# Shorter programs in a one-token attention and feed-forward block: K turned a tile at a time, head 0's scores as a loop, 1/L taken where o is gathered

## The chip, the core and the metric

The kernel runs on one core of a Trainium2 chip. The metric is the device time of one launch in microseconds, the median of several runs. Beside the times there is one profiled execution of the kernel; every stretch and every row below comes from that one.

## What is computed

One token (a row of 512 numbers) goes through a conditioned block: six modulation vectors from `silu(c) @ w_mod`, a layer norm, attention with 32 query heads over a cache of 8 key/value heads with 32768 positions each, an output projection, and a feed-forward part with ReLU. Almost all bytes are the cache: 8 heads x (K and V) x 32768 x 128 in bf16, 8 MB for each K and each V of a head.

```python
mod = (silu(c) @ w_mod).reshape(1, 6, 1, 512)
sa, ca, ga, sb, cb, gb = (mod[:, i] for i in range(6))
h = layernorm(x) * (1 + ca) + sa
q = (h @ wq) as 32 heads of 128; k, v: 8 heads, each for 4 query heads
p = softmax(q @ k.T * 128 ** -0.5); o = p @ v
x = x + ga * (o as a row of 4096 @ wo)
h = layernorm(x) * (1 + cb) + sb
out = x + gb * (relu(h @ w1) @ w2)
```

## The kernel before

**Loads.** `stream` is a list of loads, all issued in its order on SP's queue (`stream_dma`, line 154): first half of K of head 0, `w_mod`, `wq`, second half of K0, then K1, V0, K2, V1, K3, V2 and so on, at the end `wo` in four parts, `w1`, and `w2` in five parts. They land in a `ring` of three slots of 8 MB. A load is issued only when the slot's last reader has finished: V0 takes the slot of `w_mod` and `wq`, K2 that of K0, V1 that of K1, K3 that of V0; `tail_sb` (`wo`, `w1`, `w2`) takes the slot of the last K. `need(key)` makes the loads in the program up to the one asked for.

**A head.** A K of a head lies on 128 partitions in four tiles of 64 positions each per partition (`u` = 0 to 3), and each tile in two halves. `turn_k` transposes a half in 32 x 32 blocks in place on VectorE (DVE); `scores` runs eight matmuls of 512 columns on it (TensorE, PE), so 64 for a head, into two PSUM banks. The stationary operand is `qbd`, the four queries of the head laid out block-diagonally; `build_qbd` fills it with four ScalarE (ACT) copies. `softmax(g)` is a generator, whose steps are laid between other work: the maximum over the two banks, two small transposes on PE to spread the maximum, the exponentials on ACT with their sum `l_g`, the transpose of the probabilities on DVE, and 1/L (`Lexp`, `L_ps`, `Linv`). `pv` multiplies the probabilities with V: 64 matmuls a head, a loop on PE for heads 0 to 4 and half of head 5 (a section of its own, `tile_critical`), written out for the rest. `open_o` clears its PSUM tile. `blocks`, `o_cols`, `normalise` and `spread` gather o of a head into columns, multiply by 1/L, and lay it out for the output projection `project(i)`. Parts 0 and 1 of that projection (`WOROWS`) give rows, 1 matmul of 512 columns for each row of `wo_sb`; parts 2 and 3 give columns, 4 matmuls of one column each; `join_rows` turns the rows and adds them to the columns.

**Order.** PE's and DVE's programs stand in the order in which the code is written (`manual_schedule`). For head 0 all halves are turned, then scored, then its softmax is run to the end, and only behind it stand the turns of K1. From head 1 on, the turns and scores of head h stand ahead of the PV of head h - 1. For the last head, each of the two score banks has its own maximum (`bank_max`), and the PV of the head before is laid into the gaps. Eighteen `keep_clock` matmuls into a spare bank (line 631) stand between the steps of the tail.

Of the kernel before, what the change touches and what calls it, by code (L numbers as in the profile page):

```python
# [17 lines left out]
def kernel(  # L18
# [14 lines left out]
    nc = tc.nc  # L33
# [13 lines left out]
    WOP = [(0, Hkv // 2), (Hkv // 2, Hkv // 4), (Hkv - 2, 1), (Hkv - 1, 1)]  # L47
    WOROWS = 2
    LAST = Hkv - 1
# [28 lines left out]
    front = ctx.enter_context(tc.tile_pool(name="front", bufs=1))  # L78
    mask4 = front.tile([P, 32], F32, name="mask4_sb")[:, 0:REP]
    ring = ctx.enter_context(tc.tile_pool(name="ring", bufs=3))  # L80
# [113 lines left out]
    ib = ident_bf[:]  # L194
    for hp in range(4):
        h, par = hp // 2, hp % 2
        src = AP(ib.tensor, ib.offset + 64 * h + par, [[ib.ap[0][0], P], [0, 4], [2, 32]])
        nc.vector.tensor_copy(out=sel[:, hp, :].rearrange("p (a c) -> p a c", a=4), in_=src)
    QW = P + 4 * 7
# [5 lines left out]
    nc.vector.tensor_reduce(  # L205
        out=mask4, in_=ident_f[:].rearrange("p (x q) -> p q x", q=REP), op=ALU.add, axis=AX.X,
    )

    cmask, rsel = {}, {}
    for n in sorted({n * REP for _, n in WOP}):  # L210
        cmask[n] = const.tile([P, P // n], F32, name=f"cmask{n}")
        nc.vector.tensor_reduce(
            out=cmask[n][:], in_=ident_f[:].rearrange("p (c r) -> p c r", r=n), op=ALU.add, axis=AX.X,
        )
        rsel_f = const.tile([P, n], F32, name=f"rsel_f{n}")
        nc.vector.tensor_reduce(
            out=rsel_f[:], in_=ident_f[:].rearrange("p (c r) -> p r c", r=n), op=ALU.add, axis=AX.X,
        )
        rsel[n] = const.tile([P, n], BF16, name=f"rsel{n}")
        nc.vector.tensor_copy(out=rsel[n][:], in_=rsel_f[:])  # L220

# [38 lines left out]

    acc_ps = ps_acc.tile([P, REP + KT], F32)
    nc.vector.memset(acc_ps[:], 0.0)
    oT_ps, attnT_ps = acc_ps[:, 0:REP], acc_ps[:, REP:REP + KT]

# [63 lines left out]
    for u in range(2):  # L328
        for half in range(2):
            t = need(("k", 0, u))[:, 32 * half:32 * half + 32, :].rearrange("p j d -> p (j d)").bitcast(F32)  # L330
            nc.vector.transpose(out=t, in_=t)  # L331

    mod_b = two_banks("mod_ps")
    mod_ps = [row_bank(mod_b[:, i, :]) for i in range(2)]
    to_rows(mod_ps, siluT, wm_sb, 6)
# [51 lines left out]
    q_b = two_banks("q_ps")  # L387
    q_ps = [row_bank(q_b[:, i, :]) for i in range(2)]
    wq_f = wq_sb.rearrange("p kt (i h a e) -> p kt i a h e", i=2, a=4, e=32)
# [20 lines left out]
    def build_qbd(g):  # L410
        d_ap = qbd[g % 2][:]
        d_ps = d_ap.ap[0][0]
        s_ap = qrep_sb[:]
        s_ps = s_ap.ap[0][0]
        for a in range(4):
            o = AP(d_ap.tensor, d_ap.offset + (32 * a) * d_ps + 4 * 7 + 32 * a,
                   [[d_ps, 32], [QW, 4], [1, 4]])
            i = AP(s_ap.tensor, s_ap.offset + (32 * a) * s_ps + REP * g,
                   [[s_ps, 32], [Hq, 4], [1, 4]])
            nc.scalar.copy(out=o, in_=i)  # L420


    S_tiles, m_tiles, S_ps_tiles = {}, {}, {}
    PT_tiles, Linv_tiles = {}, {}
# [4 lines left out]
    def turn_k(g, u, half):  # L429

        if u == 0 and half == 0:
            S_tiles[g] = two_banks("S_ps")
            m_tiles[g] = spool.tile([P, NG], F32, tag="m2", name="m2")
# [5 lines left out]
        t = nc.vector.transpose(out=KTt.bitcast(F32), in_=KTt.bitcast(F32))  # L439
        behind_loop(t)  # L440
# [21 lines left out]

    def bank_max(g, G):
        behind_loop(nc.vector.reduce_max(out=m_tiles[g][:, G:G + 1], in_=S_tiles[g][:, G, :], axis=AX.X))

    def softmax(g):

        S_g, m2 = S_tiles.pop(g), m_tiles.pop(g)
        m_p = spool.tile([P, 1], F32, tag="m_p", name="m_p")
        if g < LAST:  # L470
            behind_loop(nc.vector.reduce_max(out=m_p[:], in_=S_g.rearrange("p g f -> p (g f)"), axis=AX.X))  # L471
        else:
            nc.vector.reduce_max(out=m_p[:], in_=m2[:], axis=AX.X)
        yield
# [26 lines left out]
        PT_tiles[g] = P_g  # L501
        Lexp = spool.tile([P, REP], F32, tag="Lexp", name="Lexp")
        nc.vector.tensor_scalar(out=Lexp[:], in0=mask4, scalar1=l_g[:], scalar2=None, op0=ALU.mult)  # L503
# [6 lines left out]
        Linv_tiles[g] = Linv  # L510

    def pv(g, us, js=range(16)):
# [5 lines left out]

        def step(u, V, PT, Vx):
            nc.tensor.matmul(o_tiles[g][:], lhsT=PT, rhs=Vx, start=False, stop=False, skip_group_check=True)  # L520

        Vf = [V.rearrange("p (s j) d -> p s (j d)", s=4) for V in Vs]
        if g < HALVED or g == HALVED and us[0] > 0:

            with tc.tile_critical() as section:
                last_loop[:] = loop[:] = [section.name]
                with nc.tensor.Fori(0, 512 - 32 * nb + 1, 32 * nb) as at:
                    for b in range(nb):
                        for u, V in zip(us, Vf):
                            step(u, V, PT_g[:, u // 2, 32 * b + 16 * (u % 2):][:, bass.DynSlice(at, 16)],  # L530
                                 V[:, :, Dh * b:][:, :, bass.DynSlice(at * (Dh // 32), Dh)])
        else:
# [29 lines left out]
    def normalise(g):  # L562
# [6 lines left out]
        nc.vector.tensor_tensor(  # L569
            out=oA[i][:, REP * (g - g0):REP * (g - g0 + 1), :],  # L570
            in0=o_g.unsqueeze(2).to_broadcast([P, REP, CH]),
            in1=cmask[n * REP][:].unsqueeze(1).to_broadcast([P, REP, CH]), op=ALU.mult,
        )
        PT_tiles.pop(g)
# [58 lines left out]
    with tc.manual_schedule(engines={mybir.EngineType.PE, mybir.EngineType.DVE}):  # L633
        build_qbd(0)
        for turn in (turn_k, scores):
            for u in range(NTILE):
                for half in range(2):
                    turn(0, u, half)
        open_o(0)
# [45 lines left out]
        spread(part_of(g - 1))  # L685
        bank_max(h, 0)
# [5 lines left out]
        bank_max(h, 1)  # L692
        soft = softmax(h)
# [129 lines left out]
```

## Time and profile before

| | |
|---|---|
| median of 3 timed runs | 354.26 us (354.23 to 354.55) |
| span of the profiled execution, first to last instruction | 352.6 us |
| the timed median less that span | 1.66 us |
| busy, share of the span | PE 79%, weight loads 32%, DVE 57%, ACT 7%, GpSimd (POOL) 1% |
| read from memory | 149.42 MB, 424 GB/s over the span |
| mean granted PE clock | 0.937 |

The profiled execution is shown by its span alone; the time around it is the difference to the timed median. Rows of a timeline have start, duration, engine, line, operation, tiles and count, and in brackets the idle time ahead and what ended it. `SPq` is the issuing of a transfer, not the transfer. PEld is the load of a stationary operand. In a row of windows stand the stretch, its length, the busy time of PE, PEld, DVE, ACT and POOL with the number of instructions, the granted clock, the share of DMA and the GB/s.

### The profile page before, as it was taken

How to read it: one execution, taken by the hardware profiler on the slowest of the kernel's cores; microseconds unless marked ns; L12 is line 12 of the kernel's file. 1: busy time of each engine (PE TensorE's matmuls, PEld its weight loads, DVE VectorE, ACT ScalarE, POOL GpSimd, SP SyncE). 2: the span in 40 equal slices, each digit the busy share in tenths (PEclk: the TensorE clock that was granted, in tenths of full speed). 3: DMA queues.
4: the chain of work that ended last, by engine and by line, in shares of the span. 5: the costliest groups of instructions: out<-in, count | busy, mean ns of one | idle time of the engine just before them, and what ended most of it. 6: DMA issues, size and time to landing. Idle time of an engine off the chain costs nothing. (4 is left out here: it accounts for less than half of the span.)

```text
span 352.6 us, 3715 instructions
## 1 busy us (share of the span) xinstructions
PE 277.9 (79%) x1310; PEld 113.5 (32%) x1310; DVE 201.0 (57%) x226; ACT 25.1 (7%) x69; POOL 3.1 (1%) x15
## 2 busy tenths in 40 slices
PE   0065891895998599976998499968999799989994
PEld 0021330331333234322333134323444233434442
DVE  6663564984079614974099506975684257744142
ACT  1200103002000200001000200011000100011000
POOL 2000000000000000000000000000000000000000
PEclk9999897798999879998999879996999989999999
DMA  9999989999999999999999999999999999999995
GB/s 357 398 435 452 472 388 461 454 394 454 461 394 448 439 424 439 424 433 439 416 446 446 409 440 461 411 394 454 431 414 435 457 417 420 444 439 409 425 425 214
DMA packets 5224, 149.59 MB, mean 424 GB/s; under 512 B 604, under 2 KB 988, under 8 KB 1628
## 3 DMA queue, kind: packets, MB, share of 16 engines
q1 hardware_dynamic: 5180, 149.43, 98.5%
q8 instruction: 8, 0.13, 0.1%
q14 instruction: 4, 0.03, 0.0%
q10 hardware_dynamic: 32, 0.00, 0.0%
HBM read 149.42 MB, written 0.00 MB: 424 GB/s over the span
## 5 line engine op out<-in xcount | busy, mean ns | idle before, releaser
L439 DVE STREAM_TRANSPOSE Ksb<-Ksb 128x2048 f32<-128x2048 f32 x60 | 133.1, 2276 | 60.2 <-DMA Ksb<-in_A_k_cache_dram 60.2
L520 PE MATMUL o_ps<-Vsb,P_g 128*16 (+1 forms) x512 | 127.0, 408 | 13.0 <-ACT P_g L495 10.0
L458 PE MATMUL S_ps<-Ksb,qbd 128*128 128x512 bf16 x512 | 120.4, 386 | 10.9 <-DVE Ksb L439 9.3
L458 PEld LDWEIGHTS <-qbd 128*128 128x128 bf16 x512 | 49.6, 98 | 78.1 <-issue 21.8
L520 PEld LDWEIGHTS o_ps<-Vsb,P_g 128*16 x352 | 34.0, 97 | 67.8 <-issue 36.5
L520 PEld LDWEIGHTS <-P_g 128*16 128x16 bf16 x160 | 13.8, 90 | 19.0 <-issue 0.4
L420 ACT COPY qbd<-qrep_sb 32x16 bf16<-32x16 bf16 x32 | 6.4, 201 | 175.2 <-PE S_ps L458 174.1
L500 DVE STREAM_TRANSPOSE P_g<-P_g 128x1024 bf16<-128x1024 bf16 x8 | 10.0, 1245 | 14.1 <-ACT P_g L495 14.1
L471 DVE TENSOR_REDUCE m_p<-S_ps 128x1 f32<-128x1024 f32 x7 | 8.6, 1223 | 13.3 <-PE S_ps L458 13.3
L322 PE MATMUL mod_ps<-wmq_sb,siluT 128*1 128x512 bf16 x24 | 3.6, 624 | 9.9 <-DMA wmq_sb<-in_w_mod_dram 9.9
L331 DVE STREAM_TRANSPOSE Ksb<-Ksb 128x2048 f32<-128x2048 f32 x4 | 8.9, 2280 | 1.6 <-DMA Ksb<-in_A_k_cache_dram 1.6
L476 PE MATMUL mT_ps<-ident_f,m_p 128*1 128x128 f32 x8 | 2.2, 270 | 8.9 <-DVE m_p L471 7.9
L495 ACT ACTIVATE P_g<-S_ps,nbias 128x1024 bf16<-128x1024 f32 x8 | 8.9, 1114 | 0.2
L506 PE MATMUL L_ps<-Lexp,ones_f 128*128 128x4 f32 x16 | 3.1, 263 | 6.3 <-DVE Lexp L503 4.3
L492 ACT ACTIVATE nbias<-Mb_ps 128x1 f32<-128x1 f32 x8 | 1.4, 171 | 88.3 <-PE Mb_ps L490 88.3
L509 DVE RECIPROCAL Linv<-L_ps 128x4 f32<-128x4 f32 x8 | 1.3, 164 | 10.9 <-PE L_ps L506 10.9
L252 PE MATMUL xc_ps<-cx_sel,wmq_sb 16*128 16x2 bf16 x4 | 0.3, 172 | 8.7 <-DVE wmq_sb L246 8.7
L555 PE MATMUL acc_ps<-mask_sb,Y 16*128 16x4 f32 x16 | 3.0, 258 | 4.9 <-DVE Y L551 4.9
L548 DVE TENSOR_TENSOR o_ps<-o_ps,smask 16x512 f32<-16x512 f32 x8 | 5.3, 668 | 2.8 <-PE o_ps L520 2.8
L586 DVE CAST o_sb<-o_ps 128x4 bf16<-128x4 f32 (+2 forms) x4 | 0.7, 165 | 10.3 <-PE o_ps L582 10.3
L506 PEld LDWEIGHTS L_ps<-Lexp,ones_f 128*128 128x128 f32 x16 | 2.6, 203 | 9.6 <-issue 5.6
L551 DVE TENSOR_REDUCE Y<-o_ps 16x128 f32<-16x512 f32 x8 | 5.4, 678 | 0.3
(116 smaller groups left out, 82.8 us busy)
## 6 DMA issues: line engine op xcount, KB each, us to landing
Ksb<-in_A_k_cache_dram SPq DMA_DIRECT2D x5, 4096.0 KB, 23.5
Vsb<-in_A_v_cache_dram SPq DMA_DIRECT2D x5, 4096.0 KB, 38.0
wmq_sb<-in_A_wq_dram SPq DMA_DIRECT2D x1, 4096.0 KB, 28.0
Vsb<-in_A_v_cache_dram SPq DMA_DIRECT2D x2, 2048.0 KB, 38.1
Ksb<-in_A_k_cache_dram SPq DMA_DIRECT2D x1, 4032.0 KB, 37.1
wmq_sb<-in_w_mod_dram SPq DMA_DIRECT2D x1, 3072.0 KB, 18.8
tail_sb<-in_A_wo_dram SPq DMA_DIRECT2D x1, 2048.0 KB, 23.0
tail_sb<-in_B_w_dram SPq DMA_DIRECT2D x1, 1792.0 KB, 30.4
```

The costliest lines, as they stand in the source:

```text
L322: nc.tensor.matmul(dst[j // 4][32 * (j % 4):32 * (j % 4) + 1, :], lhsT=src_T[:, kt:kt + 1], rhs=w[:, kt, j * 512:(j + 1) * 512], start=(kt ...
L331: nc.vector.transpose(out=t, in_=t)
L420: nc.scalar.copy(out=o, in_=i)
L439: t = nc.vector.transpose(out=KTt.bitcast(F32), in_=KTt.bitcast(F32))
L458: nc.tensor.matmul(S_ps_tiles[g], lhsT=qbd[g % 2][:, hp, 4 * (7 - s):4 * (7 - s) + P], rhs=KTv[:, 16 * sl:16 * sl + 16, h, :, par], start= ...
L471: behind_loop(nc.vector.reduce_max(out=m_p[:], in_=S_g.rearrange("p g f -> p (g f)"), axis=AX.X))
L495: nc.scalar.activation(out=P_g[:], in_=S_g.rearrange("p g f -> p (g f)"), func=ACT.Exp, bias=nbias[:], scale=scale, accum_out=l_g[:],)
L500: behind_loop(nc.vector.transpose(out=P_g[:], in_=P_g[:]))
L506: nc.tensor.matmul(L_ps[:], lhsT=ones_f[:], rhs=Lexp[:], start=True, stop=True)
L520: nc.tensor.matmul(o_tiles[g][:], lhsT=PT, rhs=Vx, start=False, stop=False, skip_group_check=True)
L548: nc.vector.tensor_tensor(out=o, in0=o, in1=smask[:].unsqueeze(2).to_broadcast([16, 4, Dh]), op=ALU.mult,)
L551: nc.vector.tensor_reduce(out=Y[:], in_=o.rearrange("p s d -> p d s"), op=ALU.add, axis=AX.X)
```

## The change

- K is turned a whole tile at a time (4096 columns of 32 bits) where it was half a tile.
- The scores of head 0 are a loop of eight steps with eight matmuls each, over all four tiles, into two banks cleared beforehand.
- 1/L is a column of 16 numbers (`L_ps` by a matmul of `mask16` with `l_g`), taken in `blocks` where o is masked; `normalise` has one product for a whole part of the projection.
- The last head has one maximum over both banks.
- `build_qbd` is one GpSimd product with a mask where it was four ACT copies.
- Part 2 of the projection gives rows too (`WOROWS` 3), ahead of `join_rows`.
- Five fillers stay of eighteen.
- `sel` is one copy for four, the casts of `rsel` go to GpSimd, two clearings of a bank become one, the written-out PV of heads 5 to 7 starts its own accumulation and needs no clearing.

```diff
-    WOROWS = 2
+    WOROWS = 3
...
     def build_qbd(g):
-        for a in range(4):
...
-            nc.scalar.copy(out=o, in_=i)
+        nc.gpsimd.tensor_tensor(
+            out=AP(d_ap.tensor, d_ap.offset + 4 * 7, [d_ap.ap[0], [QW, 4], [32, 4], [1, 4]]),
+            in0=AP(s_ap.tensor, s_ap.offset + REP * g, [s_ap.ap[0], [Hq, 4], [0, 4], [1, 4]]),
+            in1=AP(m_ap.tensor, m_ap.offset + OUT0, [m_ap.ap[0], [0, 4], [1, 4], [0, 4]]),
+            op=ALU.mult,
+        )
...
     def turn_k(g, u, half):
...
         if g == 0 and u < 2:
             return
+        if half:
+            return
+        KTt = Ksb.rearrange("p j d -> p (j d)")
         t = nc.vector.transpose(out=KTt.bitcast(F32), in_=KTt.bitcast(F32))
...
+    def scores_looped(g):
+
+        nc.vector.memset(S_tiles[g], 0.0)
+        K = pieces[f"Ksb{g}"][:].rearrange("p (b s jj h i par) -> p b h par s jj i", b=NG, s=8, jj=16, h=2, par=2)
+        with tc.tile_critical() as section:
+            last_loop[:] = loop[:] = [section.name]
+            with nc.tensor.Fori(0, 8) as at:
+                for b in range(NG):
+                    for hp in range(4):
+                        h, par = hp // 2, hp % 2
+                        nc.tensor.matmul(
+                            S_tiles[g][:, b, :].rearrange("p (o jj i) -> p o jj i", o=1, jj=16),
+                            lhsT=qbd[g % 2][:, hp, :][:, bass.DynSlice(4 * 7 - at * 4, P)],
+                            rhs=K[:, b, h, par][:, bass.DynSlice(at, 1)],
+                            start=False, stop=False, skip_group_check=True,
+                        )
...
     def softmax(g):
...
-        if g < LAST:
-            behind_loop(nc.vector.reduce_max(out=m_p[:], in_=S_g.rearrange("p g f -> p (g f)"), axis=AX.X))
-        else:
-            nc.vector.reduce_max(out=m_p[:], in_=m2[:], axis=AX.X)
+        behind_loop(nc.vector.reduce_max(out=m_p[:], in_=S_g.rearrange("p g f -> p (g f)"), axis=AX.X))
...
-        Lexp = spool.tile([P, REP], F32, tag="Lexp", name="Lexp")
-        nc.vector.tensor_scalar(out=Lexp[:], in0=mask4, scalar1=l_g[:], scalar2=None, op0=ALU.mult)
         yield
-        L_ps = small_ps([P, REP], "L_ps")
-        nc.tensor.matmul(L_ps[:], lhsT=ones_f[:], rhs=Lexp[:], start=True, stop=True)
+        L_ps = small_ps([16, 1], "L_ps")
+        nc.tensor.matmul(L_ps[:], lhsT=mask16, rhs=l_g[:], start=True, stop=True)
         yield
-        Linv = spool.tile([P, REP], F32, tag="Linv", name="Linv", bufs=3)
+        Linv = spool.tile([16, 1], F32, tag="Linv", name="Linv", bufs=3)
...
     def open_o(g):
-        nc.vector.memset(o_tiles[g][:], 0.0)
+        if g < HALVED:
+            nc.vector.memset(o_tiles[g][:], 0.0)
...
     def blocks(g):
-        nc.vector.tensor_tensor(
-            out=o, in0=o, in1=smask[:].unsqueeze(2).to_broadcast([16, 4, Dh]), op=ALU.mult,
+        nc.vector.scalar_tensor_tensor(
+            out=o, in0=o, scalar=Linv_tiles.pop(g)[:], in1=smask[:].unsqueeze(2).to_broadcast([16, 4, Dh]),
+            op0=ALU.mult, op1=ALU.mult,
         )
...
     def normalise(g):
-        o_g = oT_sb[:, REP * g:REP * (g + 1)]
-        nc.vector.tensor_tensor(out=o_g, in0=oT_ps, in1=Linv_tiles.pop(g)[:], op=ALU.mult)
...
+        if g == g0 + n - 1:
+            nc.vector.tensor_tensor(
+                out=oA[i][:], in0=oT_ps[:, REP * g0:REP * (g0 + n)].unsqueeze(2).to_broadcast([P, n * REP, CH]),
+                in1=cmask[n * REP][:].unsqueeze(1).to_broadcast([P, n * REP, CH]), op=ALU.mult,
+            )
...
         build_qbd(0)
-        for turn in (turn_k, scores):
-            for u in range(NTILE):
-                for half in range(2):
-                    turn(0, u, half)
+        for u in range(NTILE):
+            turn_k(0, u, 0)
+        scores_looped(0)
         open_o(0)
...
         project(0)
-        keep_clock(2)
         o_cols(LAST)
-        keep_clock(2)
         project(1)
         normalise(LAST)
         spread(3)
-        keep_clock(2)
         project(2)
-        keep_clock(1)
         join_rows()
         keep_clock(1)
         project(3)
...
             e = expand(x1T[:], room("tail_sb", TAIL + 1024, [P, 32, KT]).rearrange("p (m kt) -> p m kt", kt=KT))
-            keep_clock(2)
             x1_ps.append(four_rows(e, "x1"))
             keep_clock(2)
 
-        keep_clock(3)
         layernorm_T(x1T[:], stat2, h2T[:], modT_sb[:, 3 * KT:4 * KT], ncb[:], "ln2", meanwhile)
...
-        keep_clock(3)
+        keep_clock(2)
```

More of the change, by code (lines that the diff above doesn't have):

```diff
@@ L78 @@
     front = ctx.enter_context(tc.tile_pool(name="front", bufs=1))
-    mask4 = front.tile([P, 32], F32, name="mask4_sb")[:, 0:REP]
+    mask16 = front.tile([P, 32], F32, name="mask16_sb")[:, 0:16]
+    mask4 = mask16[:, 0:REP]
     ring = ctx.enter_context(tc.tile_pool(name="ring", bufs=3))
@@ L194 @@
     ib = ident_bf[:]
[L195 to L198, printed above, removed]
+    nc.vector.tensor_copy(
+        out=sel.rearrange("p (h par) (a c) -> p h par a c", h=2, a=4),
+        in_=AP(ib.tensor, ib.offset, [ib.ap[0], [64, 2], [1, 2], [0, 4], [2, 32]]),
+    )
     QW = P + 4 * 7
@@ L205 @@
     nc.vector.tensor_reduce(
-        out=mask4, in_=ident_f[:].rearrange("p (x q) -> p q x", q=REP), op=ALU.add, axis=AX.X,
+        out=mask16.rearrange("p (s q) -> p s q", q=REP),
+        in_=AP(ident_f[:].tensor, ident_f[:].offset, [ident_f[:].ap[0], [0, 4], [1, REP], [REP, P // REP]]),
+        op=ALU.add, axis=AX.X,
     )
@@ L219 @@
         rsel[n] = const.tile([P, n], BF16, name=f"rsel{n}")
-        nc.vector.tensor_copy(out=rsel[n][:], in_=rsel_f[:])
+        nc.gpsimd.tensor_copy(out=rsel[n][:], in_=rsel_f[:])
     smask = const.tile([16, 4], F32)
@@ L258 @@
     cT, xT = xc[:, 0, :], xc[:, 1, :]
-    acc_ps = ps_acc.tile([P, REP + KT], F32)
+    acc_ps = ps_acc.tile([P, Hq + KT], F32)
     nc.vector.memset(acc_ps[:], 0.0)
-    oT_ps, attnT_ps = acc_ps[:, 0:REP], acc_ps[:, REP:REP + KT]
+    oT_ps, attnT_ps = acc_ps[:, 0:Hq], acc_ps[:, Hq:Hq + KT]
     def bank(name):
@@ L328 @@
     for u in range(2):
-        for half in range(2):
-            t = need(("k", 0, u))[:, 32 * half:32 * half + 32, :].rearrange("p j d -> p (j d)").bitcast(F32)
-            nc.vector.transpose(out=t, in_=t)
+        t = need(("k", 0, u)).rearrange("p j d -> p (j d)").bitcast(F32)
+        nc.vector.transpose(out=t, in_=t)
     mod_b = two_banks("mod_ps")
-    mod_ps = [row_bank(mod_b[:, i, :]) for i in range(2)]
+    row_bank(mod_b)
+    mod_ps = [mod_b[:, i, :] for i in range(2)]
     to_rows(mod_ps, siluT, wm_sb, 6)
@@ L387 @@
     q_b = two_banks("q_ps")
-    q_ps = [row_bank(q_b[:, i, :]) for i in range(2)]
+    row_bank(q_b)
+    q_ps = [q_b[:, i, :] for i in range(2)]
     wq_f = wq_sb.rearrange("p kt (i h a e) -> p kt i a h e", i=2, a=4, e=32)
@@ L410, in build_qbd @@
     def build_qbd(g):
[L411 to L414, printed above, removed]
-        for a in range(4):
[L416 to L423, printed above, removed]
+        d_ap, s_ap, m_ap = qbd[g % 2][:], qrep_sb[:], rowpick[:]
+        nc.gpsimd.tensor_tensor(
[4 more added lines that the diff above has]
+        )
+    S_tiles, S_ps_tiles = {}, {}
     PT_tiles, Linv_tiles = {}, {}
@@ L432, in turn_k @@
             S_tiles[g] = two_banks("S_ps")
-            m_tiles[g] = spool.tile([P, NG], F32, tag="m2", name="m2")
         Ksb = need(("k", g, u))
@@ L517, in pv, with step @@
         Vs = [need(("v", g, u)) for u in us]
-        def step(u, V, PT, Vx):
-            nc.tensor.matmul(o_tiles[g][:], lhsT=PT, rhs=Vx, start=False, stop=False, skip_group_check=True)
+        def step(u, V, PT, Vx, first=False):
+            nc.tensor.matmul(o_tiles[g][:], lhsT=PT, rhs=Vx, start=first, stop=False, skip_group_check=True)
         Vf = [V.rearrange("p (s j) d -> p s (j d)", s=4) for V in Vs]
-        if g < HALVED or g == HALVED and us[0] > 0:
+        if looped(g, us):
             with tc.tile_critical() as section:
@@ L535, in pv @@
                     c0 = 32 * j + 16 * (u % 2)
-                    step(u, V, PT_g[:, u // 2, c0:c0 + 16], V[:, :, Dh * j:Dh * (j + 1)])
+                    step(u, V, PT_g[:, u // 2, c0:c0 + 16], V[:, :, Dh * j:Dh * (j + 1)], (u, j) == (0, 0))
     def open_o(g):
         o_tiles[g] = ps_o.tile([16, 4 * Dh], F32, tag="o", name="o_ps")
-        nc.vector.memset(o_tiles[g][:], 0.0)
+        if g < HALVED:
+            nc.vector.memset(o_tiles[g][:], 0.0)
     Y_tiles = {}
@@ L555, in o_cols @@
         nc.tensor.matmul(
-            oT_ps, lhsT=Y_tiles.pop(g)[:], rhs=qsel, start=True, stop=True, skip_group_check=True,
+            oT_ps[:, REP * g:REP * (g + 1)], lhsT=Y_tiles.pop(g)[:], rhs=qsel,
+            start=True, stop=True, skip_group_check=True,
         )
@@ L566, in normalise @@
         CH = P // (n * REP)
-        o_g = oT_sb[:, REP * g:REP * (g + 1)]
-        nc.vector.tensor_tensor(out=o_g, in0=oT_ps, in1=Linv_tiles.pop(g)[:], op=ALU.mult)
[L569 to L573, printed above, removed]
+        if g == g0 + n - 1:
+            nc.vector.tensor_tensor(
+                out=oA[i][:], in0=oT_ps[:, REP * g0:REP * (g0 + n)].unsqueeze(2).to_broadcast([P, n * REP, CH]),
+                in1=cmask[n * REP][:].unsqueeze(1).to_broadcast([P, n * REP, CH]), op=ALU.mult,
+            )
         PT_tiles.pop(g)
@@ L634 @@
         build_qbd(0)
-        for turn in (turn_k, scores):
-            for u in range(NTILE):
-                for half in range(2):
-                    turn(0, u, half)
+        for u in range(NTILE):
+            turn_k(0, u, 0)
+        scores_looped(0)
         open_o(0)
```

9 lines of the change are left out of this document (3 added, 6 removed).

## The prediction

> **What bounds the kernel now.** I read the page first, then the chain that ended last, then the timeline of SP's queue (which issues nearly all transfers), then the timeline of the head and of the tail, and last the windows for the granted clock. The page:
>
> ```profile
> span 352.6 us, 3715 instructions
> ...
> DMA  9999989999999999999999999999999999999995
> ...
> q1 hardware_dynamic: 5180, 149.43, 98.5%
> q8 instruction: 8, 0.13, 0.1%
> q14 instruction: 4, 0.03, 0.0%
> ```
>
> The DMA engines are busy for nine tenths and more in every slice but the last: 149.43 MB in 98.5% of the span. No compute engine is the bound; PE, DVE and ACT matter only where they hold a slot of the ring so long that the next load comes late, or after the last byte. The chain shows the second place:
>
> ```profile
> 338.44 11.14 DMA tail_sb<-in_B_w_dram
> ...
> 349.62 0.29 PE end_ps L784 x4
> ...
> 349.94 0.29 DVE o_rows L789
> ...
> 350.26 0.28 DVE o_bf L791
> ```
>
> The last w2 piece lands at 349.58, and only four matmuls, two DVE operations and the store follow. So the time is: the stream from its start to 349.58, every idle stretch of it included, then 3.0 us to the span's end, then what lies around the span: the timed median is 354.26, which is 1.66 above the profiled span. I keep both remainders. A change of compute counts only if it makes the stream idle, takes bytes out of it, or makes PE miss the landing of w1 and w2.
>
> Where can the stream idle? Where SP issues a load later than the load before it ends. SP's queue and the two places where DVE waited for K:
>
> ```profile
> 52.06 0.33 SPq L154 DMA_DIRECT2D Ksb<-in_A_k_cache_dram  x1
> 79.83 0.33 SPq L154 DMA_DIRECT2D Vsb<-in_A_v_cache_dram  x1
> 102.08 0.33 SPq L154 DMA_DIRECT2D Ksb<-in_A_k_cache_dram  x1
> 350.57 0.29 SPq L792 DMA_DIRECT2D out_dram<-o_bf  x1
> ```
>
> ```profile
> 60.18 15.47 DVE L439 STREAM_TRANSPOSE Ksb<-Ksb 128x2048 f32<-128x2048 f32 x7 [0.62 <-DMA Ksb<-in_A_k_cache_dram]
> 98.77 8.89 DVE L439 STREAM_TRANSPOSE Ksb<-Ksb 128x2048 f32<-128x2048 f32 x4 [13.13 <-DMA Ksb<-in_A_k_cache_dram]
> ```
>
> K of head 1 is down at about 60.1 and K of head 2 at 98.7, with V of head 0 between: 38.6 us for two 8 MB loads, 19.3 each. So V0 ends near 79.4, K2 at 98.7, V1 at 118.0. The three loads shown are K2 (slot of K0, free when head 0's scores end), V1 (slot of K1, free when head 1's scores end) and K3 (slot of V0, free when head 0's PV loop ends). They are issued 27, 19 and 16 us before the load ahead of them ends. From issue to the first bytes I take 1.0 us, an estimate: at least the 0.3 of the issue, at most the 2.0 from 350.57 to the span's end, in which a whole store and the closing fit. That slack is what the change spends.
>
> **The change part by part.** *Head 0's scores as a loop.* Before, the 64 matmuls start as soon as the queries stand, while the second half of K0 is still on its way:
>
> ```profile
> 36.38 15.65 PE L458 MATMUL S_ps<-Ksb,qbd 128*128 128x512 bf16 x64 [1.35 <-ACT qbd L420]
> 39.25 8.89 DVE L439 STREAM_TRANSPOSE Ksb<-Ksb 128x2048 f32<-128x2048 f32 x4 [3.89 <-DMA Ksb<-in_A_k_cache_dram]
> 52.06 1.22 DVE L471 TENSOR_REDUCE m_p<-S_ps 128x1 f32<-128x1024 f32 x1 [3.36 <-PE S_ps L458]
> 57.27 1.25 DVE L500 STREAM_TRANSPOSE P_g<-P_g 128x1024 bf16<-128x1024 bf16 x1 [3.09 <-ACT P_g L495]
> 58.44 0.19 DVE L503 TENSOR_SCALAR Lexp<-mask_sb,l_g 128x4 f32<-128x4 f32 x1
> L273 DVE MEMSET q_ps<- 128x512 f32 x2 | 1.0, 485 | 0.2
> ```
>
> After, each step of the loop takes a slice of all four tiles, so it waits until all are turned (39.25 + 8.89 = 48.1) and for a new clearing of both score banks, placed behind the turns in DVE's order (two banks at 0.485: 49.1). Entering such a section shows in the PV loop, which starts 0.6 us after the exponentials it waits for:
>
> ```profile
> 83.48 0.19 ACT L495 ACTIVATION_READ_ACCUMULATOR P_g<-S_ps,nbias 128x1 f32 x1
> 84.24 17.68 PE L520 MATMUL o_ps<-Vsb,P_g 128*16 x64 [2.02 <-ACT P_g L495]
> ```
>
> So the loop starts near 49.7. PE has then been idle since the queries (35 us), and the clock is down, as it was in the same position for head 1's scores:
>
> ```profile
> 62.97 0.14 PEld L458 LDWEIGHTS <-qbd 128*128 128x128 bf16 x1 [0.28 <-issue]
> 63.40 0.14 PEld L458 LDWEIGHTS <-qbd 128*128 128x128 bf16 x1 [0.28 <-issue]
> 66.81 6.45 PEld L458 LDWEIGHTS <-qbd 128*128 128x128 bf16 x30 [0.28 <-issue]
> 60.10:63.40 3.30, 0.81 (x3) 0.28 (x3) 3.22 (x2) 0.00 (x0) 0.00 (x0) 0.50 1.24 536
> 63.50:66.90 3.40, 3.40 (x10) 1.14 (x9) 3.40 (x3) 0.00 (x0) 0.00 (x0) 0.50 0.89 386
> 66.90:70.30 3.40, 3.40 (x17) 1.49 (x16) 3.40 (x2) 0.00 (x0) 0.00 (x0) 1.00 1.11 482
> ```
>
> The first two rows are one matmul per 0.43 us at a granted clock of 0.50, the third is 6.45/30 = 0.215 at 1.00; there the clock came back after one full window of work. I take 4.8 us at the low clock (11 matmuls) and 53 at 0.215: 16.2 us. The loop ends near 65.9 where the straight code ended at 52.0. (The skill agrees: Trainium skill, "TensorE: Matmul & The Clock Gate", Part 1, has half rate as the default after an idle window of some 3.4 us and full rate after one busy window.) From the reduction of the maximum to the turned P took 57.27 + 1.25 - 52.06 = 6.5; the 1/L step behind it shrinks (Lexp goes, its matmul has run by then; 0.16 for the reciprocal). K1's turns, which stand behind this softmax on DVE, start not at 60.2 but at 66.1 + 6.6 = 72.7.
>
> *K a tile at a time.* 64 turns become 32 of twice the size: 2.22 us for a half by the pitch of 8.89/4, so a tile takes 4.4 at most and saves at most some 0.1; K1 is turned at 72.7 + 17.7 = 90.4. But the last matmuls of a head now wait for a whole tile: 16 matmuls at 0.215 and 0.3 of latency, 3.7, where eight took
>
> ```profile
> 77.90 1.90 PE L458 MATMUL S_ps<-Ksb,qbd 128*128 128x512 bf16 x8 [0.30 <-DVE Ksb L439]
> ```
>
> So head 1's scores end at 94.1 instead of 79.8, 14.3 later. V1 is issued at 94.1, for a stream that needs it at 98.7: still in time. The softmax and PV loop behind it keep their 102.08 - 79.83 = 22.25, and K3 is issued at 116.4, its bytes come at 117.4, and V1 ends at 118.0 on the last of the sixteen engines. On the first it ends earlier: the eight instruction packets of the page are 16 KB each, and 0.1% of 16 engines' span is 5.6 us, about 0.7 us per packet on whichever engine carries it, so engines lie 1 to 2 us apart, an estimate. **The slack is gone here**: the early engines idle 0.5 to 2 us and lose their lead, and the ones that later carry instruction packets end last. I take 1.5 us. From below: at full clock the loop takes 13.8, K3 comes 2.4 earlier, and nothing idles: 0. From above: the PV loop's pace (17.68/64 = 0.276 a matmul, loop instructions included) makes it 17.7, and a longer low clock adds 1.0: K3's bytes at 119.9, 4 us of idling on the early engines. For later heads the same +1.8 per head falls into slack of the same kind, 16 us for K3 by the rows above, and PE catches up, since a head's load takes 38.6 and its PE work 64 x 0.215 + 17.7 + about 4 = 35.5.
>
> *Shorter programs.* Head 0's 64 matmuls become eight in a body (with as many weight loads, some 100 instructions less), part 2 of the output projection 4 for 16, and 13 fillers go: about 150 PE instructions. A packet less takes 0.7 us off one engine, at the end 0 to 0.5 us: 0.2. The Trainium skill, "Runtime: NRT & Kernel Launch", section on instruction fetch mechanics, has blocks of 16 KiB, 256 instructions; the row of q8 (0.13 MB in 8) agrees, and by it 150 instructions are at most one packet.
>
> *Block-diagonal queries by GpSimd*: four ACT copies per head go to one POOL operation, needed 14 us later for head 0 and a head later for the others: nothing. *1/L at o, joint oA, the 16-row L*: some 0.2 us of DVE per head, where DVE has idled for K (13.13 in the row above): nothing. *Head of the program*: sel, masks and POOL casts stand before the K0 that DVE waits for: nothing.
>
> *Tail.* The last head's scores end 1.6 later (as above), and its maximum is one reduction of 1.22 instead of 0.69 + 0.16. So PE's PV of the last head ends 2 us later, near 338.2 for 336.2. What it meets:
>
> ```profile
> 336.01 0.66 PEld L595 LDWEIGHTS <-o_sb 128*1 128x1 bf16 x16 [0.20 <-DMA tail_sb<-in_A_wo_dram]
> L631 PE MATMUL spare_ps<-qbd,ident_bf 128*128 128x512 bf16 x18 | 5.4, 381 | 0.0
> L464 DVE TENSOR_REDUCE m<-S_ps 128x1 f32<-128x512 f32 x2 | 1.4, 685 | 2.0 <-PE S_ps L458 2.0
> L473 DVE TENSOR_REDUCE m_p<-m 128x1 f32<-128x2 f32 x1 | 0.2, 155 | 0.0
> 345.30 0.93 PE L761 MATMUL hid_ps<-tail_sb,h2T 128*1 128x448 bf16 x16 [1.28 <-DMA tail_sb<-in_B_w_dram]
> 348.32 1.58 PE L784 MATMUL end_ps<-tail_sb 128*32 128x128 bf16 x36 [0.52 <-DMA tail_sb<-in_B_w_dram]
> 343.40:346.80 3.40, 2.12 (x22) 0.64 (x21) 1.26 (x6) 0.09 (x2) 0.00 (x0) 1.00 0.98 405
> ```
>
> PE had 1.28 us to spare at w1 and 0.52 at w2; eleven fillers before w1 go (11 x 0.3 = 3.3 by 5.4/18), one 0.7 turn of the rows moves behind part 2. 2.0 + 0.7 - 3.3 is not later. I take 0; what it costs if the clock falls is a rival.
>
> Sum: 1.5 - 0.2 + 0 = +1.3 us, on the profiled span 353.9, on the median 354.26 + 1.3 = **355.6 us**.
>
> **The rivals.** *K3 in time*: the loop runs at 0.215 from the start, or its sections open earlier; then nothing idles, and the packet that falls out, with up to 0.5 from the instruction packets that come at other times, gives 353.4 to 354.2, say 353.9. For it: the margin is half a microsecond on the last engine. Against: the row of head 1's cold start. Chance 0.32, of which 0.10 lies more than 0.2% below. This is the side of no loss; it decides by whether K3 is issued before about 115.5. *The loop is bound by its address instructions*: its body moves two operands per matmul by register, as the PV body does, whose pace is 0.276; were it 0.40, 64 take 25.6, 9.4 more than I took, K3's bytes at 126.8, and the stream stands 8.8 to 10.8 us: 364. Against: the PV body has the same two moving operands. Chance 0.07. *Fillers gone, clock gone*: the window before w2 was 2.12 of 3.40 busy and kept 1.00, the idle one (0.81 of 3.30) 0.50; between, no row decides. At half clock w1 and w2 take 0.93 + 1.58 more, less the 0.52 to 1.28 spare: +1.2 alone, 355.5. For it: PE waits for w1 with hardly a filler left; against: PE comes 2 us later and is denser. The same page of the Trainium skill warns of gaps over some 3.4 us; no gap here is so long. Chance 0.12. *No change in what bounds* is in the first rival.
>
> **How the numbers follow.** Forecast 0.49, in time 0.32, addresses 0.07, clock 0.12. 0.2% is 0.7 us, about what a measurement of this kernel tells from none. Slower: 0.49 + 0.07 + 0.08 of the clock case = 0.64; same: 0.22 + 0.04 = 0.26; faster: 0.10. The range: from 353.7 (in time) to 358.6 (4 us of idling and a little of the tail); the far end of the address case is left out. The forecast's own range is 355.0 to 358.3.
>
> **What would show it.** Right: K2 issued near 66, V1 near 94, K3 near 116.4, and K1's first turn near 72.7; a low DMA slice near 116 to 118; the last w2 piece near 350.9; the first score matmuls of head 0 at 0.43. Wrong: K3 issued before 115 with the landing still late (then instruction packets or the tail), or PEclk under 1.0 after 340.

## The result, and the profile after

The changed kernel takes a median of 357.15 us, the kernel before 354.38 us on the same chip (354.23 to 354.57 in six runs). The ratio is **1.0074 [1.0062, 1.0085]**: slower by about 2.6 us (2.2 to 3.0), where 1.3 had been forecast. Five of the six runs lie between 356.45 and 357.51; the sixth, 363.95, was disturbed and is not in the ratio, though it is in the median. The profiled execution is the one of 357.51, the longest of the five: its span is 355.7, with 1.8 around it, 3.1 longer than the span of before.

The page of the changed kernel, the rows that answer to those of before:

```profile
span 355.7 us, 3696 instructions
...
DMA  8999999999999999999999999999999999999993
...
q1 hardware_dynamic: 5180, 149.43, 97.8%
q8 instruction: 7, 0.11, 0.1%
```

The bytes are the same; the last slice fell from 5 to 3, so more of the end is without transfers. The timeline of SP's queue after, where each load is issued, and one row of the same view of before, which answers to the last one:

```profile
67.26 0.33 SPq L155 DMA_DIRECT2D Ksb<-in_A_k_cache_dram  x1
94.75 0.33 SPq L155 DMA_DIRECT2D Vsb<-in_A_v_cache_dram  x1
115.39 0.33 SPq L155 DMA_DIRECT2D Ksb<-in_A_k_cache_dram  x1
...
260.68 0.33 SPq L155 DMA_DIRECT2D Ksb<-in_A_k_cache_dram  x1
```

```profile
256.12 0.33 SPq L154 DMA_DIRECT2D Ksb<-in_A_k_cache_dram  x1
```

K2, V1 and K3 are issued 15.2, 14.9 and 13.3 us later than before. The delay is still 4.6 at the load of 260.68. How the first head comes to it, in the timelines of DVE and PE after:

```profile
39.38 8.77 DVE L441 STREAM_TRANSPOSE Ksb<-Ksb 128x4096 f32<-128x4096 f32 x2 [3.74 <-DMA Ksb<-in_A_k_cache_dram]
48.36 0.91 DVE L467 MEMSET S_ps<- 128x1024 f32 x1 [0.21 <-DVE Ksb L441]
51.05 16.01 PE L475 MATMUL S_ps<-Ksb,qbd 128*128 x64 [15.73 <-issue]
67.22 1.22 DVE L486 TENSOR_REDUCE m_p<-S_ps 128x1 f32<-128x1024 f32 x1 [17.42 <-PEq L469]
73.64 17.39 DVE L441 STREAM_TRANSPOSE Ksb<-Ksb 128x4096 f32<-128x4096 f32 x4
91.08 3.64 PE L460 MATMUL S_ps<-Ksb,qbd 128*128 128x512 bf16 x16 [0.34 <-DVE Ksb L441]
99.15 16.07 PE L534 MATMUL o_ps<-Vsb,P_g 128*16 x64 [2.00 <-DMA Ksb<-in_A_k_cache_dram]
```

DVE is done with clearing at 49.3, the loop starts at 51.05 and ends at 67.06, DVE has waited 17.42 for it, and only behind head 0's softmax come the turns of K1, at 73.64 where they had come at 60.18. Everything of head 1 is shifted by that.

What the stream made of it, by the windows from 96 to 126 us, where K2 ends, V1 passes and K3 begins (last two columns: share of DMA, GB/s), first before, then after:

```profile
96.00:126.00 30.00, 23.54 (x98) 9.39 (x97) 22.83 (x19) 2.18 (x7) 0.00 (x0) 0.93 1.02 442
```

```profile
96.00:126.00 30.00, 26.99 (x116) 10.95 (x117) 19.69 (x9) 1.38 (x3) 0.00 (x0) 0.94 0.99 418
```

At 442 GB/s the missing 24 x 30 take 1.6 us. DVE, which waits for K3, shows the same without windows, first before, then after:

```profile
137.47 8.89 DVE L439 STREAM_TRANSPOSE Ksb<-Ksb 128x2048 f32<-128x2048 f32 x4 [12.27 <-DMA Ksb<-in_A_k_cache_dram]
```

```profile
139.16 8.77 DVE L441 STREAM_TRANSPOSE Ksb<-Ksb 128x4096 f32<-128x4096 f32 x2 [2.74 <-DMA Ksb<-in_A_k_cache_dram]
```

K3 is down 1.7 later, and so are K4 (177.75 for 176.10) and K5 (216.30 for 214.63): what was lost by then does not come back up to there. The chain that ended last no longer has a transfer in it:

```profile
348.16 1.59 PE hid_ps L767 x14
349.75 0.97 PE spare_ps L646 x2
350.72 2.31 PE end_ps L790 x54
```

and the windows of the tail after show the granted clock (columns: stretch, length, PE, PEld, DVE, ACT, POOL, granted clock, DMA, GB/s):

```profile
341.70:345.10 3.40, 2.14 (x36) 1.25 (x37) 1.55 (x4) 0.00 (x0) 0.00 (x0) 1.00 1.01 424
345.10:348.60 3.50, 2.84 (x23) 1.25 (x24) 2.03 (x14) 0.29 (x1) 0.00 (x0) 0.51 0.97 396
348.60:352.00 3.40, 3.40 (x45) 1.62 (x35) 0.71 (x2) 0.47 (x2) 0.00 (x0) 0.50 0.28 104
...
350.50:351.00 0.50, 0.50 (x9) 0.35 (x10) 0.01 (x1) 0.27 (x2) 0.00 (x0) 0.50 0.07 23
```

and of before:

```profile
349.00:349.50 0.50, 0.50 (x14) 0.36 (x12) 0.00 (x0) 0.00 (x0) 0.00 (x0) 1.00 0.04 12
```

These are the last half microseconds in which bytes arrive; so the bytes end about 1.5 later than before. PE's last matmul ends at 353.03 where it had ended at 349.91, 3.1 later. The other 1.6 are PE's own. PE was late when it came into the tail: DVE's first step behind the PV of the last head, before, and the same step in e2, the changed kernel with all eighteen fillers, which keeps its clock, with e2's last matmuls:

```profile
336.36 0.69 DVE L548 TENSOR_TENSOR o_ps<-o_ps,smask 16x512 f32<-16x512 f32 x1 [2.80 <-PE o_ps L520]
```

```profile
340.22 0.75 DVE L563 SCALAR_TENSOR_TENSOR o_ps<-o_ps,Linv,smask 16x512 f32<-16x512 f32 x1 [2.80 <-PE o_ps L534]
350.06 1.85 PE L796 MATMUL end_ps<-tail_sb 128*32 128x128 bf16 x56
```

From that step to the end of the last matmul e2 takes 11.7 us at clock 1.00, without a wait of PE for bytes; before takes 13.55, of which 1.80 is the waiting of PE for w1 and w2. The changed kernel starts the step at 340.63 (its row stands below) and takes 12.4. With e2's 11.7 it would have ended near 352.3, an estimate: so of PE's 1.6 some 0.9 is the late start, more than the 1.8 of spare could take up, and 0.7 the half clock.

### The profile page after: what moved, and what is told of

It reads as the page before. It is cut to its first block, busy times and chain, and to the rows that moved or that the text cites. A ratio compares the mean times of both kernels' runs of the same rounds, so it can differ in the third digit from the quotient of the medians.

```text
span 355.7 us, 3696 instructions
## 1 busy us (share of the span) xinstructions
PE 270.0 (76%) x1285; PEld 111.4 (31%) x1285; DVE 196.3 (55%) x162; ACT 18.7 (5%) x37; POOL 6.0 (2%) x26
## 5 line engine op out<-in xcount | busy, mean ns | idle before, releaser
L441 DVE STREAM_TRANSPOSE Ksb<-Ksb 128x4096 f32<-128x4096 f32 x30 | 131.2, 4410 | 20.0 <-DMA Ksb<-in_A_k_cache_dram 20.0
L534 PE MATMUL o_ps<-Vsb,P_g 128*16 (+1 forms) x512 | 125.5, 404 | 12.7 <-ACT P_g L508 8.2
L460 PE MATMUL S_ps<-Ksb,qbd 128*128 128x512 bf16 x448 | 101.3, 383 | 6.8 <-DVE Ksb L441 6.8
L460 PEld LDWEIGHTS <-qbd 128*128 128x128 bf16 x448 | 42.7, 97 | 61.6 <-issue 10.6
L486 DVE TENSOR_REDUCE m_p<-S_ps 128x1 f32<-128x1024 f32 x8 | 9.8, 1223 | 46.1 <-PE S_ps L460 28.7
L475 PE MATMUL S_ps<-Ksb,qbd 128*128 x64 | 16.0, 414 | 15.7 <-issue 15.7
L520 DVE RECIPROCAL Linv<-L_ps 16x1 f32<-16x1 f32 x8 | 1.2, 145 | 27.2 <-PE L_ps L517 27.2
L475 PEld LDWEIGHTS S_ps<-Ksb,qbd 128*128 x64 | 6.6, 103 | 24.8 <-issue 18.1
L332 DVE STREAM_TRANSPOSE Ksb<-Ksb 128x4096 f32<-128x4096 f32 x2 | 8.8, 4423 | 1.7 <-DMA Ksb<-in_A_k_cache_dram 1.7
L563 DVE SCALAR_TENSOR_TENSOR o_ps<-o_ps,Linv,smask 16x512 f32<-16x512 f32 x8 | 5.8, 720 | 2.8 <-PE o_ps L534 2.8
L415 POOL TENSOR_TENSOR qbd<-qrep_sb,rowpick 128x64 bf16<-128x64 bf16 x8 | 2.3, 298 | 230.3 <-PE S_ps L460 169.6
```

The costliest lines, as they stand in the source:

```text
L460: nc.tensor.matmul(S_ps_tiles[g], lhsT=qbd[g % 2][:, hp, 4 * (7 - s):4 * (7 - s) + P], rhs=KTv[:, 16 * sl:16 * sl + 16, h, :, par], start= ...
L475: nc.tensor.matmul(S_tiles[g][:, b, :].rearrange("p (o jj i) -> p o jj i", o=1, jj=16), lhsT=qbd[g % 2][:, hp, :][:, bass.DynSlice(4 * 7 - ...
L534: nc.tensor.matmul(o_tiles[g][:], lhsT=PT, rhs=Vx, start=first, stop=False, skip_group_check=True)
L563: nc.vector.scalar_tensor_tensor(out=o, in0=o, scalar=Linv_tiles.pop(g)[:], in1=smask[:].unsqueeze(2).to_broadcast([16, 4, Dh]), op0=ALU.m ...
```

## The experiments

Two theories stood against each other: A, the stream idles (and PE stays behind) because head 0's loop makes K1's turns, and with them V1 and K3, late; B, the tail is late because fillers went and the clock fell. A ratio is to the kernel before in the same rounds.

### Which part costs the time

**e1**: the changed kernel with head 0's scores written out as before. **e4**: the kernel before with the loop alone (it keeps the half-tile turns). **e8**: e1 with the eighteen fillers.

```diff
 e1, e8 (against after); e4 is the reverse, against before
-        for u in range(NTILE):
-            turn_k(0, u, 0)
-        scores_looped(0)
+        for turn in (turn_k, scores):
+            for u in range(NTILE):
+                for half in range(2):
+                    turn(0, u, half)
```

> The changed kernel with head 0's scores written out again (tile by tile, behind the turns as in the kernel before). Theory A (the loop makes K3 late and leaves PE behind to the end): K2 is issued near 53, V1 near 81.5, K3 near 103; the last w2 lands near 349.3 instead of 350.9; PE ends its PV near 338.3 instead of 340.6; time 354.3 to 355.0. Rival B (the fillers that went, by the clock, cost the whole): the stream may end earlier, but the time stays at 356.4 or more. Rival C (turning whole tiles makes every head's scores end 1.6 later and this adds up): K3 comes in time but the time stays at 356 or more.

> The kernel before with only head 0's scores as the loop. A: loop from about 50.5 to 67, K3 issued near 114.5 to 116, the stream ends 1.0 to 1.6 later, PE's PV ends about 2.5 later with all fillers behind it; time 355.6 to 357.0. B and C: no loss from the loop, 354.1 to 354.6.

> The changed kernel with head 0's scores written out and all 18 fillers. The straight scores alone gave 354.57 (profiled: clock 0.50 from 342.6 to 349.4, the last matmul 1.0 behind the landing). If that low clock still costs something there: clock 1.00 to the end, last matmul within 0.7 of the landing, 353.9 to 354.4. If the rest of the change gains nothing and the fillers cost nothing: 354.4 to 354.7.

Measured: e1 354.57 us, 1.0006 [0.9996, 1.0016]; e4 357.36, 1.009 [1.0072, 1.0108]; e8 354.32, 1.0000 [0.9991, 1.001]. The loop alone carries the whole loss and without it nothing is lost that can be told from none. In e4, with all fillers, K3 is issued at

```profile
114.30 0.33 SPq L154 DMA_DIRECT2D Ksb<-in_A_k_cache_dram  x1
```

and in the windows from 96 to 126 us it has

```profile
96.00:126.00 30.00, 27.66 (x119) 11.20 (x119) 19.56 (x12) 1.38 (x3) 0.00 (x0) 0.94 0.98 418
```

the same 418 GB/s as after. Its four runs spread from 356.07 to 357.82, and the median lies above the expected range; the profile is of the fastest. e8 also says that the rest of the change except the fillers, the 1/L, the GpSimd queries, whole tiles, the rows of part 2 and what e8 keeps of the shorter program (it has 8 instruction packets, as before), is taken together worth nothing that can be measured.

### Is it the lateness or the loop

**e12**: the kernel before, no loop, 84 fillers on PE between head 0's scores and its softmax. **e14**: the changed kernel with its loop, but DVE turns the first two tiles of K1 while the loop runs, ahead of head 0's softmax. **e15**: e14 with eighteen fillers. **e10**: the first score bank written out, only the second a loop (`scores_looped` there takes the bank as a second argument).

```diff
 e12, against before, ahead of head 0's softmax
+        keep_clock(84)
 e14, e15, against after, behind open_o(0); turn_k skips these two
+        for u in range(2):
+            KTt = need(("k", 1, u)).rearrange("p j d -> p (j d)").bitcast(F32)
+            behind_loop(nc.vector.transpose(out=KTt, in_=KTt))
 e10, against after
-        scores_looped(0)
+        for u in (0, 1):
+            for half in range(2):
+                scores(0, u, half)
+        scores_looped(0, 1)
```

> The kernel before with one thing added: 84 filler matmuls between head 0's scores and its softmax, so that K2 is issued as before (52) but V1 and K3 come later. A: V1 near 96, K3 near 117 to 118.5, and the stream ends later by what K3 is past 113.7: 352.4 to 354; time 357.3 to 359.5, without a loop, without whole tiles and with all tail fillers. If it is the loop itself that costs (its instructions, the place of the instruction packets) and not the lateness: 354.2 to 355.0.

> The changed kernel, loop and all, with one edit: DVE turns the first two tiles of K1 ahead of head 0's softmax, in the time in which it idles beside the loop (49.8 to 67.2). A: K1's first two tiles are turned from 60.1 to 69, the softmax begins near 69, K1 is done near 85, V1 near 88.5, K3 near 109, so no stall: stream end 349.1 to 349.4, PE ends its PV near 338, time 354.2 to 355.4. B or the loop's own cost: 356.4 or more.

> The same with all 18 fillers: if the low clock in the tail is what is then left over the kernel before, 354.0 to 354.4, and clock 1.00 to the end; if the fillers are of no use, as the last one.

> The changed kernel with the scores of head 0's first bank (tiles 0 and 1) written out, the second bank's as a loop. A: the written half starts near 36.5 and keeps the clock up, the loop runs from about 50 to 58, K3 is issued near 107, in time: 354.3 to 355.2, with half of the loop's saving in program. B (the program's length or the instruction packets cost the time, not the loop's place): 355.8 or more.

Measured: e12 356.50, 1.0052 [1.0037, 1.0067], a loss, though 0.8 less than the least expected; e14 354.72, 1.0008 [0.9995, 1.002]; e15 354.36, 1.0031 [0.9999, 1.0063], where three of twelve runs, 357.89 to 359.04, widen the interval and are unexplained; e10 354.82, 1.001 [1.0001, 1.0019]. SP's queue in e12, and its window:

```profile
53.53 0.33 SPq L154 DMA_DIRECT2D Ksb<-in_A_k_cache_dram  x1
97.21 0.33 SPq L154 DMA_DIRECT2D Vsb<-in_A_v_cache_dram  x1
116.97 0.33 SPq L154 DMA_DIRECT2D Ksb<-in_A_k_cache_dram  x1
```

```profile
96.00:126.00 30.00, 26.62 (x114) 10.55 (x113) 20.78 (x15) 2.18 (x7) 0.00 (x0) 0.94 0.98 409
```

The timelines of DVE and SP in e14, and its window:

```profile
59.68 8.77 DVE L656 STREAM_TRANSPOSE Ksb<-Ksb 128x4096 f32<-128x4096 f32 x2 [9.76 <-DMA Ksb<-in_A_k_cache_dram]
109.70 0.33 SPq L155 DMA_DIRECT2D Ksb<-in_A_k_cache_dram  x1
```

```profile
96.00:126.00 30.00, 27.97 (x122) 10.67 (x119) 19.47 (x7) 0.00 (x0) 0.30 (x1) 1.00 1.02 442
```

A delay without any loop costs time (the window at 409 GB/s), and the whole loop without the delay costs nothing that shows (442, as before). This settles the cause: not the loop's work, but that K1's turns stand behind head 0's softmax on DVE and so V1 and K3 come late. All kernels but e7, in the order of K3's issue; "K3 down" is the moment when DVE's wait for K3 ends in its timeline, the profiled time is that of the one execution from which these moments come, and the ratio is that of all runs:

| kernel | fillers | V1 issued | K3 issued | K3 down | profiled time | ratio |
|---|---|---|---|---|---|---|
| before | 18 | 79.83 | 102.08 | 137.47 | 354.26 | 1 |
| e5 | 5 | 79.84 | 102.17 | 137.50 | 354.39 | 1.003 |
| e1 | 5 | 81.47 | 103.72 | 137.60 | 354.96 | 1.0006 |
| e8 | 18 | 81.60 | 103.86 | 137.75 | 354.32 | 1.0000 |
| e10 | 5 | 87.81 | 108.41 | 137.67 | 354.62 | 1.001 |
| e14 | 5 | 89.92 | 109.70 | 137.76 | 355.44 | 1.0008 |
| e15 | 18 | 90.46 | 110.21 | 137.51 | 354.63 | 1.0031 |
| e4 | 18 | 93.64 | 114.30 | 138.73 | 356.07 | 1.009 |
| e3 | 5 | 93.39 | 114.55 | 139.02 | 356.80 | 1.0074 |
| after | 5 | 94.75 | 115.39 | 139.16 | 357.51 | 1.0074 |
| e2 | 18 | 95.08 | 115.69 | 139.44 | 356.40 | 1.0093 |
| e11 | 5 | 94.47 | 116.89 | 140.31 | 358.85 | 1.0153 |
| e12 | 18 | 97.21 | 116.97 | 140.69 | 357.81 | 1.0052 |

Up to an issue at 110.2 K3 is down within 0.3 of before; from 114.3 on it is 1.3 to 3.2 late, and the later the issue, the later it is down. The edge lies between the two. It need not be K3's alone: V1, whose bytes could begin at 98.7, is issued later in the same kernels (90.5 to 93.4 across the edge), and in e12 the stream has a hole before K3 is issued:

```profile
104.00:106.00 2.00, 2.00 (x11) 0.84 (x10) 2.00 (x2) 0.00 (x0) 0.00 (x0) 1.00 0.38 164
```

(360 GB/s in the same stretch before.) No kernel moves one of the two loads alone across the edge. The medians do not follow the table beyond the edge: e11 and e12 issue K3 at the same moment and differ by 3.5 us, their profiled executions by 1.0. What else sets the timed runs is open.

### The fillers

**e5**: the kernel before with five fillers. **e2**: the changed kernel with eighteen.

```diff
 e2, against after; e5 is the reverse, against before
         project(0)
+        keep_clock(2)
         o_cols(LAST)
+        keep_clock(2)
...
         project(2)
+        keep_clock(1)
...
-        keep_clock(2)
+        keep_clock(3)
```

> The kernel before with 5 fillers of 18 and nothing else changed. A: the stream ends as before (349.3); the clock falls for one or two windows in the tail in some runs, and then the last matmul ends up to 1 us later: 354.3 to 355.2. B: 355.8 or more.

> The changed kernel with all 18 fillers. A: the stream ends as in the changed kernel (near 350.9), since no filler stands before it; the granted clock stays at 1.00 to the end, but 13 fillers of 0.22 to 0.3 us stand on a PE that is already late, so 356.0 to 357.5, at most 1 us better than the changed kernel. B: the clock was the whole loss: 354.4 to 355.2.

Measured: e5 355.29, 1.003 [1.0018, 1.0041]; e2 357.25, 1.0093 [1.0071, 1.0116]. Of the profiles, those of all kernels with five fillers (after, e1, e3, e5, e7, e10, e11, e14) have the low clock in the tail, and none of the six with eighteen has it. The tail of e2:

```profile
350.00:351.00 1.00, 0.94 (x34) 0.94 (x36) 0.00 (x0) 0.24 (x2) 0.00 (x0) 1.00 0.43 153
351.00:352.00 1.00, 0.91 (x30) 0.67 (x23) 0.05 (x1) 0.00 (x0) 0.00 (x0) 1.00 0.02 7
```

Clock 1.00, and PE ends with the bytes, yet the median is no better than after's. So at the median fewer fillers cost about 1.0 us in the kernel before (e5), nothing that can be told from none in the changed program with K3 in time (e1 against e8, 0.25), and nothing measurable with K3 late, where the runs spread over 2 us. The profiled executions of the table say more: take from the time lost what K3 is late, and 0.2 to 0.6 is left with eighteen fillers (e4, e2, e12), 1.0 to 1.8 with five (e3, after, e11). These are three single executions against three, so a cost of the half clock where K3 is late is likely and not shown. In e2's profile the stream had its shortfall elsewhere (415 GB/s from 40 to 96 us for 432 before, 437 from 96 to 126), so what this spread is made of stays open.

### Size, warmth, two loops

**e3**: the changed kernel with half-tile turns. **e11**: 44 fillers ahead of the loop, to have the clock up. **e7**: two loops, one for each bank, the first after two turns.

```diff
 e3
-            turn_k(0, u, 0)
+            for half in range(2):
+                turn_k(0, u, half)
 e11, ahead of scores_looped(0)
+        keep_clock(44)
 e7
-        for u in range(NTILE):
-            turn_k(0, u, 0)
-        scores_looped(0)
+        turn_k(0, 0, 0)
+        turn_k(0, 1, 0)
+        scores_looped(0, 0)
+        turn_k(0, 2, 0)
+        turn_k(0, 3, 0)
+        scores_looped(0, 1)
```

> The changed kernel with K turned by halves again, the loop kept. A: the loop starts and ends as in the changed kernel, head 1's scores end 1.5 earlier, V1 near 93, K3 near 114 (the edge: 115.4 cost 1.6 of stream, 108.4 cost nothing), the stream ends 0.5 to 1.5 earlier and PE ends its PV 1 to 3 earlier: 355.3 to 356.6. C (whole tiles cost in themselves, whatever K3 does): 354.3 to 355.2. If the turn's size has no part in it: 356.8 to 357.5.

> The changed kernel with 44 more fillers on PE ahead of head 0's loop, so that the clock is up when the loop starts. A: the loop starts at the same place and ends 1.7 to 3.4 earlier, K2 near 64.5, K3 near 113, the stream ends about 1 to 1.5 earlier, time 355.2 to 356.3. If the low clock at the loop's start costs nothing, because the loop is bound by its own instructions: 356.5 to 357.5.

> The changed kernel with head 0's scores as two loops, one for each bank: the first over tiles 0 and 1 before tiles 2 and 3 are turned, the second behind them. A: the first runs from about 37.5 to 47 beside the turns, the second from about 50 to 59; K3 is issued near 108, in time; stream end 349.3, time 354.4 to 355.4. B: as the changed kernel, 356.4 or more. If entering a section costs more than the work it takes out of the way, K3 is issued later than 112 and the time is over 355.8.

e3: 356.89, 1.0074 [1.0056, 1.0092]. V1 comes 1.4 and K3 0.8 earlier than after, still beyond the edge; nothing is gained that shows.

e11: 360.02, 1.0153 [1.0136, 1.017], slower than after. Its PE timeline and the first window of its loop:

```profile
36.10 12.39 PE L646 MATMUL spare_ps<-qbd,ident_bf 128*128 128x512 bf16 x44 [0.83 <-POOL qbd L415]
50.95 15.78 PE L475 MATMUL S_ps<-Ksb,qbd 128*128 x64 [2.45 <-issue]
98.87 17.86 PE L534 MATMUL o_ps<-Vsb,P_g 128*16 x64 [2.00 <-DMA Ksb<-in_A_k_cache_dram]
```

```profile
51.00:54.40 3.40, 3.40 (x11) 1.30 (x12) 0.00 (x0) 0.00 (x0) 0.00 (x0) 0.63 1.11 482
```

The fillers ended at 48.5, PE stood 2.45 us, and the clock was down again in the loop's first window, as in these of the changed kernel:

```profile
51.00:54.40 3.40, 3.35 (x8) 1.22 (x9) 0.00 (x0) 0.00 (x0) 0.00 (x0) 0.50 0.93 405
57.80:61.20 3.40, 3.40 (x17) 1.50 (x16) 0.00 (x0) 0.00 (x0) 0.00 (x0) 1.00 1.25 540
```

So the warm loop wasn't made, and its price isn't known. The PV loop of head 0 took 17.86, and K3 came 1.5 later than after.

e7: 375.53, 1.0598 [1.0575, 1.0621]; the expectation of a gain failed. The page's DMA row and SP's queue:

```profile
DMA  8990089999999999999999999999999999999995
```

```profile
47.26 1.45 SPq L155 DMA_DIRECT2D Ksb<-in_A_k_cache_dram  x4
```

Four loads, among them the second half of K0, were held back to 47.26, when the first loop was done; after, the same four are issued from 2.12 on. The engines stand for two slices, some 20 us. This kernel tells nothing on K3.

## Why the prediction was right and wrong

**The bound** was right in its cause: issues that come late cost time. e12 and e14 show it with the lateness put in and taken out by itself. In the profiled execution the stream is half of the loss; the other half is PE in the tail.

**The way to K3** was right, step by step: K2 near 66, measured 67.26; K1's turns at 72.7, measured 73.64; V1 at 94.1, measured 94.75; K3 at 116.4, measured 115.39. The loop started 1.35 later than worked out (51.05 for 49.7) and took 16.01 for 16.2, with 8 matmuls in its first window at a clock of 0.50 and some 16 per window at 1.00: the cold start is there. The PV loop of head 0 took 16.07 and not 17.68, which brought K3 1.0 before its forecast and, by luck, hid the late start.

**The edge was misplaced.** The prediction put the bytes of K3 1.0 behind its issue, V1's end at 118.0, and said of the rival "K3 in time" that it decides by whether K3 is issued before about 115.5. K3 was issued at 115.39, and e4's at 114.30, and both lost; e15's at 110.21 was the latest that showed no idling in its profile. If the edge is K3's, and not V1's, it is 1.2 us or more, and perhaps 5, earlier than that line. The size of the term, +1.5, agrees with the profiled execution (1.7 at K3, about 1.5 at the last bytes), but by luck: by the prediction's own line an issue at 115.39 should have cost nothing, and it took a K3 put 1.0 too late and an edge put too late as well to arrive at 1.5. In the timed runs the size is not settled: e4, the loop with all else as before, lost 3.2 at the median and 1.8 in its profiled run, its fastest. The bounds 0 to 4 held both. Of the signs, the low DMA slice near 116 to 118 is not in the page's forty slices, and PEclk under 1.0 after 340, named as a sign of being wrong, came.

**The tail, taken at 0, failed.** It cost 1.6 in the profiled execution, half of the whole. The profile after, PE's and DVE's timelines:

```profile
340.63 0.75 DVE L563 SCALAR_TENSOR_TENSOR o_ps<-o_ps,Linv,smask 16x512 f32<-16x512 f32 x1 [2.80 <-PE o_ps L534]
344.30 0.24 PE L633 MATMUL acc_ps<-tail_sb,place 128*32 128x4 f32 x8 [0.82 <-DVE tail_sb L628]
348.09 1.66 PE L767 MATMUL hid_ps<-tail_sb,h2T 128*1 128x448 bf16 x16
```

Two terms of "2.0 + 0.7 - 3.3" were wrong. PV of the last head ends at 340.6, not near 338.2, which is where it does end with K3 in time (338.1 in e1, 337.8 in e8). "PE catches up" was true but small: from 115.39 to 260.68 are four heads of 36.3 us against 38.6 of loading, so of 13.3 us 4.6 were left. And the fillers that go (twelve ahead of w1, not eleven) do not give back 3.3: from the first row to the matmuls on w1 are 7.5 us here, 8.1 in e2 with all fillers and 7.7 before without its wait, so 0.2 to 0.6 are gained, with the half clock from 345.1 on in it. The second row suggests why: PE waits there for DVE, so what stood in its place was in part free. "Fillers gone, clock gone", set at 0.12 as a rival, came true beside the forecast: half clock from 345.1 to 352.0. It was a rival in the text, but the two exclude each other in nothing; by its price of 1.2 the sum would have been 2.5. That this makes the timed 2.6 is not shown, since e2 has its clock and takes as long.

By the Trainium skill, "TensorE: Matmul & The Clock Gate", Part 1, the clock falls to half after an idle window of some 3.4 us. The trace doesn't agree with that as a limit: the window before the clock fell, 341.70 to 345.10, had PE busy 2.14 of 3.40, and the longest gap there was 0.82.

**What was costed at nothing** and was nothing, taken together: the queries by GpSimd, 1/L at o, the head of the program, whole tiles (e8, 1.0000 [0.9991, 1.001]). The 0.2 for the packet that goes (7 for 8 in the page) is not tested by e8, which has 8; e14 and e15 have 7, and no gain shows in them (1.0008 and 1.0031). The rival of address instructions (0.40 a matmul) fell: 16.01 for 64 is 0.25, cold start included.

No version that was run beats the kernel before; e8 and e15 equal it at the median.

## What to carry to other kernels

When work is put into a loop, price the wait for all of its inputs and what stands behind it in the order of each engine, rather than its instructions: here 64 matmuls cost what they had cost, but the transposes queued behind them on another engine came 13.5 us late, and reordering those (e14) gave nearly all of it back. Here an issue of K3 3.7 us ahead of the moment when the mean of the stream needed it was already late, and one 7.8 ahead was not; so keep more slack than the mean says. Look too at how long an engine waits for its last bytes (1.8 us here): if it is late by more than that when it comes to them, time is lost though the bytes are there. And list rivals that can come true together as sums, not as alternatives.

## What was not expected of the hardware

- A PE busy for 2.14 of 3.40 us lost its clock, where the kernel before had kept it with 2.12 of 3.40 in 343.40 to 346.80. The busy time by the profile doesn't decide it.
- The same PV loop of 64 matmuls takes 16.0 to 17.9 us: 17.68 for head 0 before, 16.07 after, 17.86 in e11, with the granted clock at 0.57 to 0.59 in the first 4 us and at 0.99 or more from then on in all three. It moved K3 by 1.6 us, more than most of the terms of the sum; its cause is open.
